# A new written order, engine choice and buffer layout for a four-layer attention kernel

## The chip, the core and the metric

The kernel runs on one core of a Trainium2 chip. The core has five engines that run side by side, each with its own in-order list of instructions: PE (matrix products; its weight loads are listed as PEld), ACT (ScalarE, the only one here that computes exponentials), DVE (VectorE), POOL (GpSimd) and SP (SyncE, which here only issues transfers). An engine waits for another through semaphores. [...] The metric is the device time of one execution in microseconds (us). The kernel before has a median of 419.46 us in three runs (419.31 to 419.74).

## What is computed

Four residual layers on an input of 2048 rows and 512 columns, two kinds of attention in turn, 32 heads of width 16:

```python
x = A_x
x = x + _A_ref(_layernorm(x), A_wqkv, A_wo)
x = x + _B_ref(_layernorm(x), B_wqkv, B_wo)
x = x + _A_ref(_layernorm(x), A_wqkv, A_wo)
x = x + _B_ref(_layernorm(x), B_wqkv, B_wo)

# _A_ref: linear attention
phi = lambda t: jnp.where(t > 0, t + 1, jnp.exp(t)) + 1e-6
kv = einsum("bhsd,bhse->bhde", phi(k), v); z = phi(k).sum(s)
o = einsum(phi(q), kv) / (einsum(phi(q), z) + 1e-6)

# _B_ref: softmax attention over the last 256 positions
scores = q @ k.T * Dh**-0.5, masked to 0 <= i - j < 256
o = softmax(scores) @ v
```

Each kind ends in a product with its `wo`.

## The kernel before

The rows are cut into 16 tiles of 128. A step for one tile is an operation: `s.op(name, {engine: cost}, function, ...)`, which records what it reads and writes. There are 2762 of them on the fast path, and each becomes one instruction or a short run of instructions on one engine. Their names begin with the stage and end with the step.

- `1.` is the key and value half of layer 1: layer norm (`ln.st`, `ln.ag`, `ln.ae` and `ln.xn` on DVE, `ln.rs` on POOL), a transposition `ln.xT`, projections of k and v on PE (`k0`, `k1`, `v0`, `v1`: two halves each), the feature map (`k.e` and `k.r` on ACT, `k.m` and `k.a` on DVE), a copy `vc` of v out of PSUM, and `kv`, the sum over tiles. The transpositions of tiles 0 to 3 run on PE (L834), the others as transfers that SP issues (L827), of 128 KB each.
- `2.` and `3.` are the query halves of layers 1 and 3: `q0`, `q1`, the feature map, the products `n0`, `n1`, the division (`da`, `dr`, `dm` on DVE, L950 to L953), a transposition `o.oT`, the output projection `o.w0`, `o.w1` and the addition `o.x`.
- `2.b.` and `3.b.` prepare layers 2 and 4: layer norm, projections of k, q and v, and copies out of PSUM. A key tile goes out twice, masked for two halves (`kb0`, `kb1`, into kbd, L970), a query tile once (`qc`, into qT, L844), a value tile once (`vc`, into vt, L844); POOL then moves vt into vbd by transfers (`vd0`, `vd1`, L980).
- `2.a.` and `3.a.` are the attention of a tile: products of scores at the border of the window (`sH`, L1006) and inside it (`s0` to `s3`, L1055), their exponentials on ACT (`eH`, L1034; `e00` to `e31`, L1076), masks on DVE (`mH`, L1042; `m0` to `m3`, L1094), products with values (`u`, L1112 and L1124), the division (`dr0`, `dm0` and so on, L1134 and L1136), and the output projection. The last tile of layer 4 has its own ending (`z...`, in `b_end`). `zb` there writes a scaled identity over a part of the zero tile, from which `warm` and `warm2`, products on zeros at the start, read their operands.
- `2k.` is the key and value half of layer 3, worked on while layer 2 still runs.

Most copies out of PSUM may run on ACT or on DVE; the operation lists both. [...]

The order is written out by hand, as it were, in `ORDER`, one word an operation: its number; an apostrophe if it runs on the second engine of its list; and, after a colon, the slots of the buffers that it opens (for PSUM, the bank). `schedule` walks through the words. An engine's instructions stand in the order in which its operations stand there, so the words also fix the sequence in SP's list of transfers and in POOL's. It also adds up a planner's time from the costs in `s.op`; a buffer without a written slot would be placed by it. `emit` then works out the semaphore waits.

Each engine runs a first block of instructions and then branches to a second (`jump`, L504), at the place that `ORDER` gives it.

The loads are issued in `loads` (L774): x tiles and w_Aq on SP, w_Ak and w_Av on ACT, then w_Ao, w_Bk, w_Bq, w_Bv and w_Bo (512 KB each) on SP, at the place in SP's list that `ORDER` gives them.

Of the kernel before, what the change touches and what calls it, by code (L numbers as in the profile page):

```python
# [8 lines left out]
ACT = mybir.ActivationFunctionType  # L9
# [9 lines left out]
ONE = 2.0 ** -9  # L19
# [299 lines left out]
def _act_cost(n):  # L319
    return 0.055 + 0.000833 * n  # L320
# [29 lines left out]
933 476:3 477:3 939:1 672:5.1 673 962:6.0.2 961 686:4.0 963 964 700 487:2.3 488 701 674' 934 702:3 687 688 689 489 490 491:0 492:0 940:5 941 942 943:0  # L350
1019:0.6.2 1020 1021 501 944 690:3.2 691 987 478:2 954:0.4.0 955 956 692' 953 1022 479 678 1416:3.1 1417 716 993:0.6.4 1418' 911:5 912 965 994 995 480 913
1419 966:0.3.5 703:3 967 711:2.2.0 502:6.1 945:1 660 661 957 503 504 505 493:5 494 495 968 969 712 713 997:0.3.1 998 999 506:2 970:5 975:2 971 1054:0.6.0 717
718 719 734 735 972 976 977 1055 1056 752 753 989:0.3.0 679 990 973:2 974:3 978:3 979 1000 704:5.1 988 705 706' 707' 736 708:2.3 737 996 709 710' 714 991 992
1028:0.6.3 1029 1030 1420 1421 720:1 507:3 508:4 1422 693:5.1.1 694 695' 1001:0.2.2 1002 1003 509 510 946:7 947 948 1032:0.5.5 1033 1005:4 1006 1004 1423:2
980:2 1034 738:0 511:7.12.1 1010:3 1433 1434 1435 1007 721:2 1008:0 1009:0 1089:0.5.1 981:2 982 1090 1091 1058 1436 512 1424:0 696 697 515 513 1437:3 770
1411:4.1.0 1412 983 1447 1448 1449 1450 1024:0.5.0 1025 1026 1011 1012 1013:1 1014 1031 726:7.0 727 728' 1413 1414 1415 1063:0.2.4 722:6.2 723 1451:1 1027
# [3 lines left out]
1465 1062 514 740:5.3 741 1075:4 1076 1077 715 1050:3 1092 742 743 1460' 1101 1102:0.2.1 1430:7.2 1103 1104 1431 733 1456 1457 1070 1074 1080:6 1078:0 1079:2  # L360
1159:4.0.0 1160 1161 1432' 747:7.1.2 748 1466 1467:3 749' 1081 1094:2.4.0 1095 1096 1162 1468:3 1082 1083:1 762:7.2 763 1084 1105 764' 773 774:0 1133:0.2.4
1134 1135 516 1085:1 1051:6 1097 1052 1053 765:7.2.4 1477 1106:0.4.2 1107 1108 766 767' 768 758:6.4 759 760' 761' 1137:0.2.5 1138 1139 775:3 1110:7 1111 1109
517:4.2 518 519 520 1112 1113:3 1114:3 1115:6 521:0 1194:0.2.1 1195 1196 1086:7 1087 541:5.13.2 542 545 543 1116 1129:0.2.0 1130 1127 1131 1163 1088 750 751
1136 1491 776:7.5 777 1128 778' 526:5.14.3 527 530 1117 779' 1168:0.2.3 522:2 780:7.3 1118:0 1119 1120:0 528 1132 529 531 781 782' 1478 1479 1480 523:6 524
525 788 1492 789 790 1140 1169 1170 1141:0.4.1 1145:7 1142 1146 1143 1144 1147 1148:1 791 792:1 1149:1 1493 1172:0.2.2 1474:6.7 1469:5.7.0 1475 1173 1476'
793:1 1174 1175 1470 1471 1472 1150:4 769 1229:0.2.2 1230 1231 1121:7 1122 1473 1151 1494 1495:2 1496:4 1481:3 1482:7 1164:0.5.0 1123 1152 1505 1153:3 1154
1171 1165 1166 1167 783:3.0.5 784 532:0.2 794:2.0 1155:3 533 534 535 536:2 1198 1506 1507 1203:4.6.4 785 801:3.1.1 802 803' 1204 1205 1206 795 796 797' 1180:5
1176:0.6.5 1508 1181 1177 556:4.15.1 557 1178 558 1233 1179 1197 560 798:3.0 799 800' 1207:0.6.1 1208 1209 1182 1183:0 1184:0 1185:4 1186 1264:0.2.0 1265 1266
1187 544 546 1188:1 1189 537:1 538:7 539 540 806 1199:0.5.0 1200 1201 807 808 1156:4 1157 1497:7.3.3 1158 1498 1499 1238:0.2.3 1239 1240 1690:6.16.0 1691
1502:5.3 1694 1692 809 810:0 1503 1500 1501 1504' 1202 1190:2 1191:7 1192 1193 1211:0.2.2 1212 1213 1483:5.4.2 1484 1215:4 1521 1242:0.6.5 1243 1244 1216 1217  # L370
811:2 819:3.2.0 1210 1535 1214 1218:3 547:0.2 1219:3 548 559 1536 549 1537 550 551:1 552:0 1485 812:2.1 813 814 815 561 820 821 816:4.1 817 1486 1232 1487
1509:1 1510:9 818' 1234:0.6.0 1235 1538 1539:2 1220:2 1705:3.17.3 1241 1236 1237 1706 1221 1222 1223:0 1224 1709 786 1540:8 2716 1273:0.4.4 1274 1461:7.6 1462
# [995 lines left out]
```

## Time and profile before

| | us |
|---|---|
| median of three runs | 419.46 |
| span of the profiled execution, first to last instruction | 417.1 |
| PE busy | 401.3 |
| ACT busy | 383.3 |
| DVE busy | 379.2 |
| POOL busy | 106.7 |

The profile holds one execution. It gives the span, from the first instruction to the last; the time of a run has some 2.4 us more than that. A group line reads: line of the kernel, engine, operation, what is written and read, shapes, count; then busy time and mean ns of one; then the engine's idle time just before them and what ended it. A line of the view by stage reads: the stretch, its length, then the busy time of PE, PEld, DVE, ACT and POOL with the number of instructions, the clock that PE was granted (1.00 is full), the share of the transfer engines and GB/s. A line of waits reads: who waited, for whom, us in total, times, longest. A line of the chain reads: start, us, what. A line of the timeline reads: start, us, engine and line, what, and in brackets the idle time before it with what ended it. The line of an issue of transfers reads: what, where issued, count, KB each, median us from issue to landing. [...]

### The profile page before, as it was taken

What the parts mean: (1) busy time and instruction counts of PE and PEld (TensorE: products, weight loads), DVE (VectorE), ACT (ScalarE), POOL (GpSimd) and SP (SyncE); (2) the same over time, 40 slices, a digit from 0 to 9 for tenths busy, and PEclk for the clock granted to TensorE, in tenths of its full rate; (3) what the DMA queues carried; (4) which work ended last, traced back from release to release, by engine and by line L of the source; (5) the groups of instructions that cost most, each with busy time, mean ns of one, the idle gap of its engine ahead of it and who ended that gap; (6) DMA issues with size and microseconds to landing.
All of it is one profiled execution on the core that took longest, in us unless ns stands there. A gap on an engine that the chain in (4) does not pass through costs nothing.

```text
span 417.1 us, 18964 instructions
## 1 busy us (share of the span) xinstructions
PE 401.3 (96%) x8402; PEld 283.5 (68%) x8402; DVE 379.2 (91%) x998; ACT 383.3 (92%) x499; POOL 106.7 (26%) x202
## 2 busy tenths in 40 slices
PE   8999999999999999999999999889999999999997
PEld 3654776765767686776686677567676676677775
DVE  6999899999999999999898899999999998979784
ACT  4977979999999999999999677899999999999996
POOL 2331024521343022124150101161333113404100
DMA  8436435343243222324112201331445253243142
GB/s 273 135 63 166 113 53 123 75 55 61 54 77 51 40 48 48 41 53 85 35 40 57 43 2 39 65 81 32 81 66 82 50 72 63 55 85 54 38 93 79
DMA packets 76808, 29.48 MB, mean 71 GB/s; under 512 B 66352, under 2 KB 74672, under 8 KB 76720
## 3 DMA queue, kind: packets, MB, share of 16 engines
q1 hardware_dynamic: 71424, 22.63, 27.0%
q0 software_dynamic: 4096, 4.46, 5.8%
q8 instruction: 68, 1.11, 1.2%
q10 hardware_dynamic: 1200, 1.11, 0.8%
q14 instruction: 20, 0.16, 0.1%
HBM read 6.29 MB, written 2.10 MB: 20 GB/s over the span
## 4 chain that ended last, share of the span: by engine, by line
ACT 47%; PE 41%; DVE 10%; issue 1%; DVEq 0%
ACT pF L1076 33%; PE ps L857 17%; ACT pH L1034 9%; PE ps L869 8%; PE ps L1055 4%; PE ps L1124 4%; PE ps L1112 2%; PE ps L915 2%; ACT kbd L970 2%; DVE o L953 1%; DVE xres L892 1%; DVE stats L813 1%; ACT E L878 1%; PE ps L1253 1%; ACT vt L844 1%
## 5 line engine op out<-in xcount | busy, mean ns | idle before, releaser
L1076 ACT ACTIVATE pF<-ps 128x1024 bf16<-128x1024 f32 x240 | 231.0, 1095 | 2.7 <-PE ps L1055 2.0
L817 POOL TENSOR_TENSOR rstd<-mv,const 128x1 f32<-128x1 f32 x64 | 39.7, 622 | 208.9 <-DVE mv L816 200.1
L980 POOL DMA_DIRECT2D vbd<-vt x128 | 67.0, 532 | 81.1 <-DVE vt L844 61.6
L1034 ACT ACTIVATE pH<-ps 128x1024 bf16<-128x1024 f32 (+1 forms) x64 | 60.5, 1032 | 3.1 <-PE ps L1006 3.0
L1124 PE MATMUL ps<-vbd,pF 128*128 128x34 bf16 x1856 | 59.6, 178 | 0.0
L1124 PEld LDWEIGHTS ps<-vbd,pF 128*128 128x128 bf16 x1856 | 52.9, 96 | 3.3 <-issue 0.2
L1055 PE MATMUL ps<-qT,kbd 32*128 32x128 bf16 x1920 | 49.0, 216 | 4.4 <-ACT pF L1076 1.2
L1094 DVE TENSOR_TENSOR pF<-pF,const 128x512 bf16<-128x512 bf16 (+2 forms) x116 | 46.7, 414 | 4.8 <-ACT pF L1076 4.6
L878 ACT ACTIVATE E<-ps 128x512 bf16<-128x512 f32 x64 | 39.5, 635 | 8.4 <-PE ps L857 4.3
L813 DVE BATCH_NORM_STATS2 stats<-xres 128x6 f32<-128x512 bf16 x64 | 43.8, 687 | 1.9 <-DMA xres<-in_A_x_dram 1.1
L1055 PEld LDWEIGHTS ps<-qT,kbd 32*128 32x128 bf16 x1920 | 28.7, 92 | 22.8 <-ACT pF L1076 9.4
L1042 DVE TENSOR_TENSOR pH<-pH,const 128x1024 bf16<-128x1024 bf16 (+1 forms) x64 | 40.8, 650 | 0.0
L857 PE MATMUL ps<-w_Bv,xT 128*128 128x512 bf16 (+2 forms) x152 | 35.7, 346 | 0.3 <-ACT vt L844 0.2
L869 PE MATMUL ps<-xT,w_Bk 128*128 128x128 bf16 x512 | 35.3, 219 | 0.3
L869 PE MATMUL ps<-xT,w_Bq 128*128 128x128 bf16 x512 | 35.2, 219 | 0.1
L857 PE MATMUL ps<-w_Ao,oT 128*128 128x512 bf16 (+2 forms) x144 | 34.5, 356 | 0.7 <-ACT pF L1076 0.6
L1112 PEld LDWEIGHTS ps<-vbd,pH 128*128 128x128 bf16 x928 | 28.6, 96 | 8.8 <-issue 1.8
L857 PE MATMUL ps<-w_Ak,xTa 128*128 128x512 bf16 (+1 forms) x134 | 33.6, 369 | 0.6 <-ACT xTa L844 0.5
L869 PE MATMUL ps<-xTa,w_Aq 128*128 128x128 bf16 x512 | 33.9, 219 | 0.2
L1112 PE MATMUL ps<-vbd,pH 128*128 128x34 bf16 x928 | 32.9, 178 | 1.1 <-ACT pF L1076 0.3
L857 PE MATMUL ps<-w_Bo,oT 128*128 128x512 bf16 (+2 forms) x140 | 33.0, 355 | 0.7 <-ACT pF L1076 0.6
L857 PE MATMUL ps<-w_Av,xTa 128*128 128x512 bf16 (+2 forms) x133 | 33.6, 371 | 0.0
(95 smaller groups left out, 622.4 us busy)
## 6 DMA issues: line engine op xcount, KB each, us to landing
vbd<-vt POOLq DMA_DIRECT2D x128, 34.0 KB, 2.1
xres<-in_A_x_dram SPq DMA_DIRECT2D x16, 128.0 KB, 4.9
out_dram<-xres SPq DMA_DIRECT2D x15, 128.0 KB, 1.9
oT<-o SPq DMA_TRANSPOSE x60, 2.6
w_Ak<-in_A_wqkv_dram ACTq DMA_DIRECT2D x1, 512.0 KB, 4.8
w_Av<-in_A_wqkv_dram ACTq DMA_DIRECT2D x1, 512.0 KB, 5.8
w_Aq<-in_A_wqkv_dram SPq DMA_DIRECT2D x1, 512.0 KB, 6.2
w_Ao<-in_A_wo_dram SPq DMA_DIRECT2D x1, 512.0 KB, 4.0
```

Of the source, the lines that this page charges most:

```text
L813: s.op(n + ".st", {"DVE": 0.595}, lambda e, en: e.bn_stats(a_st, x.h[:]), reads=[x], writes=[st])
L857: i = e.matmul(g.h[:, a:b], xT.h[:, kt, :], w.h[:, kt, a:b], start=(kt == 0), stop=(kt == 3), skip_group_check=True)
L869: i = e.matmul(g.h[:, f * P:(f + 1) * P], w.h[:, kt, f * P:(f + 1) * P], xT.h[:, kt, :], start=(f == 0 and kt == 0), stop=(kt == 3), skip_ ...
L878: s.op(n + ".e", {"ACT": _act_cost(512)}, lambda e, en: e.activation(E.h[:], g.h, ACT.Exp, bias=0.0), reads=[g], writes=[E])
L980: return [e.dma_start(vbd.h[64 * a:64 * a + 64, j, a], vt.h[64 * j:64 * j + 64, a]) for j in range(2)]
L1034: return e.activation(d, c, ACT.Exp, bias=0.0, scale=DH ** -0.5)
L1042: return e.tensor_tensor(v, v, tr, ALU.mult)
L1055: i = e.matmul(ss[r // 2].h[:, r % 2, k * P:k * P + P], kbds[fj[m] // 2].h[32 * r:32 * r + 32, f, fj[m] % 2, :], qT.h[32 * r:32 * r + 32, ...
L1076: s.op("e%d%d" % (u, g), {"ACT": _act_cost(1024)}, lambda e, en, S=ss[g], pb=pb, g=g: e.activation(pb.h[:, 2 * g:2 * g + 2, :], S.h, ACT.E ...
L1094: return e.tensor_tensor(v, v, tr, ALU.mult)
L1112: i = e.matmul(U.h[:, c:c + 34], pH.h[:, 4 * r + f, 64 * a:64 * a + P], vbds[j // 2].h[:, j % 2, :, 4 * f + r, :], start=first[0], stop=Tr ...
L1124: i = e.matmul(U.h[:, c:c + 34], pFs[at[f, m][0]].h[:, r, at[f, m][1] * P:at[f, m][1] * P + P], vbds[fj[m] // 2].h[:, fj[m] % 2, :, 4 * f ...
```

## The change

The operations and what they compute stay. `ORDER` is written anew, all 2762 words, after a local search on a replay of the schedule:

```diff
 ORDER = """
-4 2 37 38 66 6 0 61:7 1 7 8 9 41 68 42 43 44 45 69 70 46 5 3 71 72:0 73:6.0 47 62 67 39 40 74 85 86 87 88 10 75:7.0.0 76 11 12 89:1 33 25 90:6.1 91 13 102
...
-2717:3 2726 2660 2661 2695 2696 2751:7.3 2697 2734 2735 2736 2743 2745 2744 2589 2752 2753 2755 2756 2754 2758 2759 2757 2760 2761
+0 6 7 1 5 3 67 4 2 39 37 8 9 38 66 41 42 43 44 61:7 45 46 47 48 49 68 69 70 40 71 72:0 85 35 73:6.0 62 33 50 51 52 53 54 55 56 57 58 59 74 75:7.0.0 86 87 88
...
+2755 2754 2758 2759 2756 2757 2760 2761
 """
```

Three costs and one dependency change beside it:

```diff
-        s.op("dr", {"DVE": 0.17}, lambda e, en: e.reciprocal(dn.h[:], dn.h[:]), writes=[dn], tail=0.11)
+        s.op("dr", {"DVE": 0.275}, lambda e, en: e.reciprocal(dn.h[:], dn.h[:]), writes=[dn])
...
-            s.op("kb%d" % a, {"ACT": _act_cost(512), "DVE": _dve_cost(512)}, kb, reads=[gk, self.mab], part=[kbd])
+            s.op("kb%d" % a, {"ACT": 0.57, "DVE": 0.659}, kb, reads=[gk, self.mab], part=[kbd])
...
-        s.op("zb", {"DVE": 0.2}, lambda e, en: e.tensor_scalar(big.h, self.ident.h[:], LIFT / ONE, None, op0=ALU.mult), reads=[self.ident, self.zero], writes=[big])
+        zb = s.op("zb", {"DVE": 0.2}, lambda e, en: e.tensor_scalar(big.h, self.ident.h[:], LIFT / ONE, None, op0=ALU.mult), reads=[self.ident, self.zero], writes=[big])
+        for d in s.ops:
+            if d.name in ("warm", "warm2"):
+                zb.deps[d] = False
```

(`_act_cost(512)` is 0.48 and `_dve_cost(512)` 0.598.)

What the new list does, read from the two lists engine by engine:

- Of PE's 975 operations 804 stand at another place, most by a few places (median 2, farthest 28); of DVE's about 990, 898 (median 6, farthest 378: `zb`, from the middle of the kernel to its first stage).
- 27 copies go from ACT to DVE and 21 from DVE to ACT; ACT has 497 operations instead of 503, DVE 999 instead of 993.
- 487 of 687 placements in PSUM banks differ, and 443 others.
- SP's list: before, the four loads of w_Ao, w_Bk, w_Bq and w_Bv stand behind the twelve transpositions of stage `1.` that SP issues; after, they stand ahead of them, right behind the last load of an x tile. w_Bo stands behind the first five of these transpositions instead of behind the first transpositions of `2.`.
- The branch of DVE stands 42 operations before its end instead of 12; POOL's is its 29th operation instead of its 110th; ACT's stays near its 295th.
- PE changes between row groups and square products 304 times instead of 302.

More of the change, by code (lines that the diff above doesn't have):

```diff
@@ L352 @@
[L352 to L355, printed above, removed]
@@ L363 @@
[L363 to L366, printed above, removed]
@@ new lines @@
+886 605' 403:7 404 418:6 915 65 865:0.2.0 426 405 864 419 644 631:3 632:7.3 633 916 420 634' 866 867 892:0.4.1 639:6.2.5 427:2.3 428 640 893 894 635' 442:0.1
[4 rows of a table added]
+919:0.5.0 926 882 1405 986 930 448:4 449 920 958:2.0.3 921 1406 675:7.2.2 676 672:6.1 959 960 450 931:2.4.1 932 677' 673 472:0.2 473 922 698 474 933 935:7 475
[3 rows of a table added]
+753 713' 1054:0.6.0 754 1055 502:2.0 503 976 1421 734 704:5.1 705 1056 977 504 505 506:2 735 989:0.2.0 990 991 706' 693:7.1.4 694 978:3 707' 946:6 979
+1028:0.4.3 1422 679 947 695' 1423:1 1029 736 708:7.3 709 992 1001:0.2.2 507:2 948 996 1030 1002 1003 508:6 509 710' 1005:7 1032:0.4.5 1000 1433 510 1004 1006
@@ new lines @@
+1007 720:0 1010:6 1033 1034 1008:1 1009:1 1434 1435 1022 770 771 1424:1 1057 980:1 1089:0.2.1 714 981:7 982 1090 1091 1011 1024:0.4.0 1012 755 737 772 1031
+1023 1013:2 511:3.12.2 512 983 1014 721:2 1436 1437:3 1447 1025 1026 729:2.2.0 730 731' 1063:0.4.4 722:7.2 723 1411:6.6.3 515 513 1027 1064 1065 1015:3 1438:2
+1036:0.2.1 1037 1412 756:2 1448 1449 726:5.0 727 1425:4.5.0 1426 1413 1038 1427 738:1 724' 725' 1414 1415 1039 1040:7 1067:0.2.2 773 1439:6.4.1 1450 732 1440
+1041 1068 728' 1035 1428 1069 696 733 1045:5 1451:0 1441 1042 1429 1043:0 1124:0.2.2 715 697 757:4 1046 1125 1126 1442 514 1443 739:0 1444:4.7 1445 1044:0
@@ new lines @@
+1070 1047 1452:5 1066 1059:0.6.0 1060 1061 1446' 744:3.1 1016:2 1017 1048:3 1049 1058 1098:0.4.3 1093 1099 1100 745 1018 746' 1128 1463 1464 1050:0 740:7.3
+741 1062 1453:6.2.3 742 743' 1071:0.2.5 1072 1073 1458:5.3 1459 1465 1454 1460' 1075:4 1455 1076 1102:0.2.1 1466 1103 1074 1456 1457 1077 1078:1 1079:2 516
+1104 1080:7 1081 1159:0.5.0 1160 1082 765:4.2.5 766 1083:2 1105 1084 1467:3 1161 1094:0.2.0 767' 1095 1096 1163 1430:7.2 1085:2 762:6.2 1101 1092 1431
+1133:0.4.4 1134 763 747:3.0.1 748 1135 1051:2 749 750 751 1052 1106:0.4.2 1097 1432' 764' 774:2 1468:4 775:1 517:6.0 1053 518 1107 1108 758:3.4 759 1110:2
@@ new lines @@
+1111 760 519 520 521:3 1137:0.6.5 1138 1139 1112 1477 1109 1115:5 1116 1478 761' 1194:0.3.1 1113:3 1479 1114:1 1136 522:1 1195 1117 1162 1118:1 1119 780:2.3
+781 1196 523:7 1129:0.5.0 524 782 1120:3 1130 1140 1086:4 1087 1168:0.2.3 1131 1480 525 788 1088 1169 1170 776:7.5 1481:1 777 1482:3 1469:6.1.0 1141:0.4.1
+1470 541:3.13.1 789 1132 778' 779' 1127 542 783:2.1.2 784 1142 1471 1143 1491 1472 790 785' 1492 791 1145:7 1144 792:0 1473 1172:0.4.2 1146 1147 1148:2 543
+545 1197 1149:0 786 1198 1173 1174 526:3.14.3 527 1150:2 1493 1494 787 1151 1229:0.4.2 530 528 1152 1121:3 1122 1230 1231 1175 1164:0.6.0 1165 544 768 1153:0
@@ new lines @@
+1154 529 1171 1495:3 1123 556:2.15.2 1474:5.1 1475 531 1203:0.3.4 557 1166 1476' 1204 558 1205 1505 532:6.3 533 793:3 1496:8 534 535 798:5.0 799 794:1.0 795
+1155:0 1506 536:2 1176:6.3.5 801:0.0.4 537:1 802 1177 1178 1507 800' 1167 560 1180:5 1181 1182 1508 796' 797' 1179 1207:6.3.1 803' 1183:1 1184:3 1208 1232
+1185:2 1186 1187 1188:2 1264:0.6.0 1189 1509:2 1190:2 538:5 539 1206 1209 1265 1502:4.5 1199:0.2.0 540 806 807 1503 1266 1156:5 1157 1200 1201 1238:0.6.3
+1504' 804 546 769 805 1191:4 1192 1158 1239 1240 1497:5.7.0 1498 1210 1202 1215:3 1211:0.6.2 1499 1521 808 1193 1483:2.3.3 1212 1213 1705:4.16.1 1706 1216
@@ new lines @@
+1217 1707 1709 1242:0.6.5 1484 1522 1243 1510:6 1244 1500 809 1535 810:1 1523 1536 811:2 1501 1537 547:4.0 548 559 1218:3 1219:1 1524 1538 561 1690:3.17.0
+1214 549 1691 1692 1694 1485 819:1.1.3 820 1220:0 550 551:0 552:3 1234:4.6.0 812:3.1 1221 813 1222 1233 821' 1539:0 1235 1236 1486 1487 1273:4.1.4 1540:7 1274
+1223:1 1241 1275 1461:7.6 1224 814' 816:0.1 562:4.2 563 1245 817 1225:1 1462 815 564 565 553:1 1246:2.6.1 554 818 1226:0 1227 1237 1247 1248 1525:3 566:2
+1299:2.4.1 555 824 1511:1.0.2 1512 1780:7.0.3 1781 1228 825 826 1526:13 567:0 1250:6 1251 822 823 827 1549 1300 1301 1513 1550 1693 1514 1515 1551 1277:2.4.2
@@ new lines @@
+1933 2199 1959 1742 2200 1901' 2203:0.2.0 1960 2182 1945:0 1743 1744 1745:2 1934 2204 2205 1961 1962:2 1928:7.0 1929 1930' 1732:6 2207:0.4.1 2208 2209 1963:4
+1733 1931' 1734 2214 1935:3.0.4 1936 1756:0.0 1757 1758 2206 1759 1950:2.3 1746:0 1976 1937 1760:3 2243:4.6.4 1964:3.1 1902 2244 2245 1965 2230:4.0.0 2231
+2232 1951 1952 1921 1903 2183:7 1747:6 1748 2184 2185 2188:5 2189 2190 1761:2 1966' 2202 1977 1967' 1978 2210 2233 2235:0.3.2 2236 2186:2 2201 2191:1 1979
+1938 1749 1939 2187:0 2192 1946:2.2 1947 2239:0.6.5 2237 1948' 1949' 2240 2241 1968:5.0 2215:4 1969 2234 2266:2.0.1 2216 2217 1762:7 1763 2238 1970' 2242
@@ new lines @@
+2218:3 2219:1 2267 1980:1 1873 1764 2279:2.5.0 1981:3 2268 2280 2281 2251:4 1845 2252 2253 2254:0 2255:2 2247:0.2.2 2012 2248 2249 1994 1953:7.1.0 1771:5.2
+1772 1773 2246 1971:4.2.1 2193:3 1995 1954 1955 1956 2013 1972 2271:0.2.5 2250 1774 2256:7 2257 2272 2273 2258 1775:3 1973' 1858 2259:1 2275:0.5.4 1982:4.3
+1983 1996 2260 2270 2276 2277 2220:7 2302:0.2.0 2303 1984' 1985' 2304 1997 2221 2222 2223:3 2224 1776:1 1777:6 1778 2315:0.4.2 2316 2317 2014 1957 2015 2274
+1779 1986:7.1 1987 2283:2.0.1 2269 2284 2285 1988' 1860 2318 1786:6.0 1787 1788 1789 2225:0 1790:0 1989:5.0.3 2226:4 1990 1791:2 1801:2.2 1802 1991 2278
[4 rows of a table added]
@@ new lines @@
+2387:0.2.5 2388 2389 2068 2027' 2328:4 2300 2049 2354 2050 2010 2033 2069 1831:6.1 1832 2028 1833 1834 1835:3 2018:5.5 2019 2020 2377 2021 2329 2330 2331:3
+1836:0 2379:0.2.2 2380 2342 1822:7 1823 2332 2029 2011 2381 2022:6.3 2355:0.4.0 2346 2034:2 1824 2350 2023 1837:3 1838 2024' 2382 2356 2357 2410:0.6.0 2051
[4 rows of a table added]
+1869 2400:4 2401 2427:0.2.5 2414 2402 2403:1 2428 2426 2462 2404 2058:7.1 2059 2451:0.5.4 2369:1 1881:2 2060' 2429 2449 2450 2087 2431:4 2432 2433 2434:3 2452
+2105 2106:3 2107:2 2453 2405:0 2455:0.2.0 2456 2457 2076:7.2 2077 1882:6 2435:3 2430 2078' 2482:0.4.1 1883 2138 2088:2 1884 2061:7.2.0 2062 2483 2484
[4 rows of a table added]
@@ new lines @@
+2507:0 2502 2526 2112:3.0 2529 2408 2113 2114' 2535:0.4.0 2536 2537 2508:2 2509 2510 2567:0.6.2 2557 2521 2568 2569 2373 2441:2 2161:0 2108:3.4 2109 2511:0
+2512 2538 2100 2082 2083 2110' 2544:2 2559:0.4.3 2125:4 2409 2545 2560 2570 2561 2133:7.2.2 2130:6.1 2131 2132' 2111 2101 2477:1 2134 2563:0.4.4 2564 2546
+2565 2135' 2530 2334:3 2335 2558 2336 2143:3 2513:0 2566 2603:0.6.0 2604 2539:5 2540 2590:0.3.1 2541 2605 2151:7.0.5 2562 2547:2 2542:1 2543:2 2548 2591 2592
+2152 2153' 2154 2136 2571:0.5.1 2115:2.1.4 2116 2572 2117' 2594 2126:7.5 2595:0.3.5 2127 2575:2 2573 2576 2596 2597 2599:0.5.3 2577 2128' 2129' 2144:7.0 2145
@@ new lines @@
+2578:3 2606 2579:3 2574 2600 2626:0.3.0 2601 2146' 2147' 2148:2.2 2149 2580:5 2627 2639:0.6.4 2581 2593 2150' 2598 2602 2137 2628 2442:4 2640 2582 2583:0 2641
+2607:0.2.2 2549:3 2608 2443 2609 2630 2584 2444 2118 2478:7 2479 2642 2631:0.5.1 2632 2119 2611:4 2612 2613 2337 2635:0.2.5 2633 2610 2480 2636 2514:7
+2169:6.2.0 2170 2637 2614:1 2615:1 2585:2 2515 2662:0.4.2 2155 2171 2663 2664 64 2162:3.2 2163 2516 2164' 2616:2 2675:0.6.3 2617 2618 2676 2634 2677 2165'
+2619:2 2629 2620 2643:4.0.0 2166:3.3 2167 2644 2645 2550:2 2638 2168' 2667:4.6.2 2551 2647:3 2665 2666 2668 2669 2648 2445 2621:1 2671:0.4.1 2552 2672 2673
[3 rows of a table added]
```

53 lines of the change are left out of this document (8 added, 45 removed), and 94 rows, old and new, of the table ORDER.

## The prediction

> **What bounds the kernel now.** I read the page's busy times first, then busy times by stage, then the waits and the chain.
>
> ```profile
> PE 401.3 (96%) x8402; PEld 283.5 (68%) x8402; DVE 379.2 (91%) x998; ACT 383.3 (92%) x499; POOL 106.7 (26%) x202
> 0.00:58.50 58.50, 56.14 (x466) 33.26 (x467) 52.47 (x175) 44.24 (x77) 12.68 (x29) 1.00 0.50 136
> 58.50:222.30 163.80, 159.73 (x3593) 114.81 (x3594) 154.51 (x394) 160.26 (x201) 48.06 (x89) 1.00 0.32 59
> 222.30:263.60 41.30, 40.49 (x650) 29.15 (x649) 37.93 (x107) 31.80 (x52) 3.99 (x6) 1.00 0.21 40
> 263.60:417.08 153.48, 144.97 (x3698) 106.27 (x3698) 134.24 (x325) 147.04 (x170) 42.00 (x78) 1.00 0.36 66
> ```
>
> Columns two to six of a stage are its length and the busy times of PE, PEld, DVE, ACT and POOL. I cut at the first border product (L1006) of layer 2, at that of its last tile, and at the first of layer 4. In stage one PE sets the pace, in stage two ACT (160.3 of 163.8 us) with PE at its heels, in the handover PE with DVE, in the last stage ACT again. No engine has an eighth of the span to give away on average, but each stage has a different tightest one, so each shift of work is priced in its stage.
>
> ```profile
> PEld ps L1055 <- ACT pF L1076: 9.4, 34, 0.5
> PEld ps L1006 <- ACT pF L1076: 3.9, 12, 0.8
> PEld ps L1055 <- ACT pH L1034: 2.9, 11, 0.6
> PEld ps L941 <- ACT pF L1076: 2.7, 7, 0.5
> ```
>
> These are PE's weight loads waiting for exponentials: 64 waits of 0.3 us, 18.9 us in all. The order can win only what lies in such short waits.
>
> ```profile
> 7.03 1.02 PE ps L857 x4
> ...
> 12.98 0.22 PE ps L834 x4
> 13.20 0.86 PE ps L857 x4
> 14.06 0.89 PE ps L869 x16
> 14.96 2.69 PE ps L857 x12
> 17.65 0.47 PE ps L915 x8
> ```
>
> From 12.98 to 18.12 the chain is PE piece after piece without a gap: any hole made in PE in stage one is paid in full.
>
> **The change, part by part.** *Copies.* 27 copies go from ACT to DVE and 21 back. Counted between the same cuts in the two orders, stage two loses 5 kbd copies and 3 plain ones (qT, vt, vA together) on ACT.
>
> ```profile
> 197.07 0.98 ACT vA L844 x2
> 201.72 1.14 ACT kbd L970 x2
> L970 DVE TENSOR_SCALAR kbd<-ps,const 128x512 bf16<-128x512 f32 x40 | 28.2, 742 | 0.5 <-PE ps L869 0.4
> L844 DVE CAST qT<-ps 128x512 bf16<-128x512 f32 x22 | 15.0, 682 | 0.9 <-PE ps L869 0.8
> ```
>
> Back to back on ACT a kbd copy takes 0.57 us and a plain one 0.49: 5 x 0.57 + 3 x 0.49 = 4.3 us less. On DVE each costs at most its mean of one, 0.74 and 0.68. DVE's net gain there is only about 1.5 us, because other DVE work leaves the stage; 154.5 + 1.5 still fits under 160.
>
> *PE pieces.* Stage two also loses two half projections (L857, 0.86 for four matmuls, so 0.43 a half) and three value products of 16 matmuls; the handover gets those five and gives half a query projection (L869, 0.89 for 16, so 0.45) to the last stage.
>
> ```profile
> 216.23 0.81 PE ps L1124 x32
> ```
>
> A value product is 0.40, so stage two loses 2 x 0.43 + 3 x 0.40 = 2.1 us of PE work and the handover gains 2.1 - 0.45 = 1.6. ACT could shorten stage two by 4.3, PE by 2.1; I take the middle, -3.2. The handover is PE's: +1.6. The last stage gets one exp and one relu of a query and one copy more on ACT, less a small one, about +1.1 by 0.49 each, and 0.45 on PE; ACT is idle 6.4 us there, so +0.9.
>
> *Weight loads.* This decides. Before, SP issued twelve transposes, then the loads of w_Ao, w_Bk, w_Bq and w_Bv. After, those four stand right behind the last load of xres and ahead of every transpose (w_Bo follows five transposes).
>
> ```profile
> 9.92 0.43 SPq L774 DMA_DIRECT2D xres<-in_A_x_dram  x1
> xres<-in_A_x_dram SPq DMA_DIRECT2D x2, 128.0 KB, 4.3
> 12.29 1.30 SPq L827 DMA_TRANSPOSE xTa<-xn  x1
> xTa<-xn SPq DMA_TRANSPOSE x1, 4.1
> 36.14 0.58 SPq L774 DMA_DIRECT2D w_Ao<-in_A_wo_dram  x1
> 37.87 0.51 SPq L774 DMA_DIRECT2D w_Bv<-in_B_wqkv_dram  x1
> w_Ao<-in_A_wo_dram SPq DMA_DIRECT2D x1, 512.0 KB, 4.0
> w_Bv<-in_B_wqkv_dram SPq DMA_DIRECT2D x1, 512.0 KB, 6.3
> q1 hardware_dynamic: 71424, 22.63, 27.0%
> ```
>
> The issue costs little: four loads take 36.14 to 38.38 = 2.2 us of SP, and between 10.35 and 12.29 SP is empty. The transfer is another matter. The last xres lands at 9.92 + 4.3 = 14.2. The four weights land at 40.1 to 44.2, three steps in 4.1 us, 1.36 us each, so behind xres they end at 14.2 + 4 x 1.36 = 19.6. All of SP's transfers share one queue: 22.6 MB in q1 only fits if the transposes are in it with loads and stores. Does a transpose wait behind a bulk load there? The nearest case is w_Bo:
>
> ```profile
> 65.50 0.57 SPq L774 DMA_DIRECT2D w_Bo<-in_B_wo_dram  x1
> w_Bo<-in_B_wo_dram SPq DMA_DIRECT2D x1, 512.0 KB, 4.8
> 66.13 2.31 SPq L827 DMA_TRANSPOSE oT<-o  x1
> oT<-o SPq DMA_TRANSPOSE x1, 4.6
> xTa<-xn SPq DMA_TRANSPOSE x27, 2.6
> ```
>
> w_Bo lands at 70.3. The transpose issued right behind it, at 66.1, took 4.6 us instead of the usual 2.6 and landed at 70.7, 0.4 later; the first of all, behind xres, took 4.1 and landed at 16.4, 2.2 after xres. So I take the queue to be in order. [...] Behind four loads the first transpose lands at 19.6 + 0.4 to 19.6 + 2.2, so 20.0 to 21.8. It carries tile 4, whose first projection stands in the new order behind 15 half projections of k or v, 6 of q, three L834 groups and one L915 group: 15 x 0.43 + 6 x 0.45 + 3 x 0.22 + 0.24 = 10.05 us after the first k projection, which starts at 7.03, so due at 17.1. PE is empty for 2.9 to 4.7 us. Some comes back: PE sits without work for 2.4 of stage one's 58.5 us now, and DVE, which it waits for there, runs ahead meanwhile. I take +3.3, inside the lower half for that; bounds 0 (transposes pass the loads) and +4.7.
>
> *At nothing.* The new durations of dr, kb0 and kb1 only feed the planner, whose order, engines and banks are written out: no instruction. zb (0.19 us) moves into stage one, where DVE has 6 us idle; with that cover gone, 0.2. The new waits for warm and warm2 hold nothing: both stand ahead of PE's first projection at 7.03. Two more changes between square and row-tiled matmuls:
>
> ```profile
> L1055 PEld LDWEIGHTS ps<-qT,kbd 32*128 32x128 bf16 x1920 | 28.7, 92 | 22.8 <-ACT pF L1076 9.4 <-issue 4.7 <-ACT pH L1034 2.9
> ```
>
> 22.8 us over 120 groups is 0.19 each, hidden or not: 0.2 at most.
>
> *DVE's branch* moves from 12 to 42 DVE instructions before the end, with o.x and the last kbd copies queued behind it and PE's scores waiting for those.
>
> ```profile
> L504 DVEq COMPARE_BRANCH  x1: 53/53/53, 407.2 to 407.2; - x1
> 407.14 0.42 DVE L1136 SCALAR_TENSOR_TENSOR o<-dn,ps 128x256 bf16<-128x256 f32 x1
> 410.12 0.21 DVE L1175 RECIPROCAL dn<-ps 128x8 f32<-128x8 f32 x1 [2.56 <-PE ps L1166]
> 388.00:394.00 6.00, 5.90 (x142) 3.84 (x140) 4.27 (x9) 6.00 (x8) 0.00 (x0) 1.00 0.18 46
> ```
>
> The branch takes 0.05 us, the hole after it is 2.56 and is put down to PE, so its price lies between 0.05 and 2.6. DVE is idle 1.7 of 6 us at the new place; 0.9 could stick out. I take 0, since the hole has another releaser. [...]
>
> *Order as such.* 804 of PE's 975 steps and 487 of 687 bank placements differ. No row prices this. The 18.9 us of short waits bound it: a fifth won is -3.8, a sixth lost +3.2. I take -1.5, nearer the middle than either, on the gain side because the kbd copy that the old plan held for 0.48 us reads 0.57, and work planned behind it had to come late.
>
> Sum: +3.3 - 3.2 + 1.6 + 0.9 - 1.5 = +1.1 on a span of 417.1. The median 419.46 is 2.4 above that span, and I leave this part as it is: 419.46 + 1.1 = **420.6 us**.
>
> **Rivals.** *The transposes pass the weight loads.* Then the 3.3 falls out: 417.3. For it: one late transpose near w_Bo coincides with POOL's transfers too. Against: 22.6 MB in one queue.
> *PE takes the loss back.* PE's order has enough tile-0-to-3 work, stage two falls by the full 4.3 and the waits by 3: 3.3 - 4.3 + 1.6 + 0.9 - 3.0 = -1.5, 418.0. For it: ACT's 160.3 of 163.8.
> *It evens out.* Hole 2.8 instead of 3.3, waits -2.2: -0.1, 419.4.
> *DVE becomes the bound in the handover.* Already it is busy 37.9 of 41.3 there, and 3.3 us of DVE work (layer norm steps, two kbd copies, adds) come in. If DVE sets that stage, +3.3 stands for +1.6 and stage two gains only PE's 2.1: 3.3 - 2.1 + 3.3 + 0.9 - 1.5 = +3.9, 423.4. It decides once DVE's idle time there, 3.4, is used up. [...]
>
> **Chances.** Forecast 0.40, DVE bound 0.10, evens out 0.16, PE takes it back 0.16, transposes pass 0.18. Within 0.2% (0.84 us, about what can be told apart here) is 418.6 to 420.3. So slower 0.50, same 0.16, faster 0.34. Range 416.2 to 423.4; the forecast's own, by the hole's 2.9 to 4.7 and 1 us of order to either side, 419.2 to 423.0.
>
> **What would show it.** Right: after some 17 us PE idles about 3 us, put down to the transpose's DMA or to DVE; w_Ao is issued at 10.4; the first transpose lands past 20; stage two is 2 to 4 us shorter, the handover longer. Wrong: PE stays full from 10 to 46 us (then 417.3), or the hole after DVE's branch holds up scores near 390, or DVE reads 99% in the handover.

## The result and the profile after

The changed kernel takes 433.27 us (median of four runs, 432.76 to 434.14) against 419.6 for the kernel before on the same chip: a ratio of 1.0327, 95% interval 1.0309 to 1.0345. The forecast was 420.6, range 416.2 to 423.4. Slower was right; the size was not nearly. The profiled execution's span grows from 417.1 to 431.2, by 14.1 us. (The later runs of the kernel before list spans of 417.0 to 419.5 us, 1.3 below their times, so a stage's change of less than about 1 us can lie between executions.)

The page of the changed kernel, its busy times, its granted clock by slices and its chain by engine:

```profile
PE 395.5 (92%) x8325; PEld 285.9 (66%) x8395; DVE 376.4 (87%) x1004; ACT 381.5 (88%) x493; POOL 108.2 (25%) x202
...
PEclk9979999999999999999999999999999999999998
...
PE 38%; ACT 29%; DVE 19%; DMA 11%; issue 2%; SPq 1%; DVEq 0%
```

PE, ACT and DVE are busy a little less than before and each has a smaller share. (PE's record lacks 77 matmuls, 8325 of 8402, so its busy time is understated.) A new owner stands in the chain: transfers, with 11%. The same kernel by stage, cut at the same four PE products as in the prediction (columns as there):

```profile
0.00:64.20 64.20, 57.71 (x464) 34.55 (x472) 49.56 (x173) 45.58 (x79) 13.11 (x29) 0.95 0.53 132
64.20:227.90 163.70, 153.51 (x3513) 113.86 (x3541) 153.52 (x394) 156.84 (x194) 47.58 (x85) 1.00 0.32 56
227.90:270.80 42.90, 41.45 (x689) 30.50 (x698) 39.93 (x113) 30.11 (x49) 5.58 (x10) 1.00 0.21 37
270.80:431.20 160.40, 142.88 (x3673) 106.99 (x3698) 133.38 (x327) 149.00 (x172) 41.97 (x78) 0.99 0.33 64
```

| stage | before | after | change | forecast |
|---|---|---|---|---|
| one | 58.5 | 64.2 | +5.7 | +3.3 |
| two | 163.8 | 163.7 | -0.1 | -3.2 |
| handover | 41.3 | 42.9 | +1.6 | +1.6 |
| last | 153.5 | 160.4 | +6.9 | +0.9 |
| order as such, all stages | | | in the above | -1.5 |

Where PE waits points to why. The view of waits of the changed kernel (who waited, for whom: us in total, times, longest); the line numbers are one higher than before:

```profile
PEld ps L858 <- DMA oT<-o: 10.3, 13, 1.6
PE ps L858 <- DMA oT<-o: 5.9, 8, 1.6
PEld ps L858 <- DMA xTa<-xn: 4.6, 2, 4.3
PE ps L858 <- DMA xTa<-xn: 3.8, 1, 3.8
PEld ps L870 <- DMA xT<-xn: 3.4, 3, 1.6
PE ps L870 <- DMA xT<-xn: 3.0, 3, 1.4
```

PE's matmuls wait 5.9 + 3.8 + 3.0 = 12.7 us for SP's transposes (PEld's lines are mostly the same waits, seen by the weight loads). In the kernel before there is not one such line. All lines of PE in this view add up to 28.5 us, against 10.1 before, 18.4 more; its waits for ACT shrink from 5.3 to 2.8 meanwhile. Another 5.9 of the 28.5 read "issue", against 0.2 before. Those look like gaps in the record rather than waits: the traces of this case that hold 8312 to 8326 of PE's matmuls all have 4.3 to 6.1 us of them, those that hold 8394 to 8402 at most 1.6. So the changed order won some of what the forecast had looked at, and lost more elsewhere.

The transposes themselves hardly changed. The view of tile oT, on the kernel before and then on the changed one (duration of the issue in ns, smallest, median, largest; then who waited; then issue to landing):

```profile
L827 SPq DMA_TRANSPOSE oT<-o x60: 1188/1192/2665, 46.1 to 407.6; - x60
...
who waited for it (us, times):
...
DMA to landing us min/median/max: 2.4/2.6/5.2
```

```profile
L828 SPq DMA_TRANSPOSE oT<-o x60: 1188/1264/2636, 54.1 to 419.9; - x60
...
who waited for it (us, times):
  PEld ps L858: 10.3, 13
  PE ps L858: 5.9, 8
...
DMA to landing us min/median/max: 2.4/3.0/5.1
```

In both kernels the fastest of oT lands after 2.4 us and the slowest after 5.1 or 5.2. Of all 117 transposes 37 took over 3.3 us before and 44 after: about a third, whichever order. What differs is how closely PE follows. Matched one by one in the trace, from the landing to PE's first weight load that reads it, one transpose in 117 was used within 0.35 us before, 24 after; the median margin fell from 3.2 to 2.4 us. The planner's time (`LAT["SP"]`) makes a transpose readable 1.45 us after its issue of about 1.25 has ended, 2.7 in all. A search on that time may place PE's step at exactly 2.7. Of the 117, 72 before and 64 after land within 1.45 us of the end of their issue; for the others the margin must pay. The planner's own time shows the packing. Added up by `schedule` from each kernel's words and costs, it is 412.9 us for the kernel before, where no transpose is planned to be read within 0.35 us of becoming readable, and 408.7 for the changed kernel, where 19 are. It is 408.7 with the loads at either place, so it knew nothing of the queue either.

What goes with a late landing can be read from the packets in the trace. Beside SP's queue the page lists one of instruction transfers, packets of 16 KB (queue, packets, MB, share):

```profile
q8 instruction: 68, 1.11, 1.1%
```

In the kernel before, one of these was under way between 1.0 and 2.4 us after the issue of 44 transposes; 32 of these 44 took over 3.3 us, of the other 73 only 5. In the changed kernel it is 36 of 52 with one and 8 of 65 without. Over all fifteen traces of this case it is 494 of 691 with, and 80 of 1039 without. This is a coincidence in time: no run changed the instruction transfers.

In stage one the forecast hole is there. SP's timeline of the changed kernel, and PE's:

```profile
10.90 0.43 SPq L775 DMA_DIRECT2D w_Ao<-in_A_wo_dram  x1
...
12.48 0.92 SPq L775 DMA_DIRECT2D w_Bv<-in_B_wqkv_dram  x1
14.08 9.55 SPq L828 DMA_TRANSPOSE xTa<-xn  x5
```

```profile
7.78 1.04 PE L858 MATMUL ps<-w_Ak,xTa 128*128 128x512 bf16 x4 [0.66 <-DMA w_Ak<-in_A_wqkv_dram]
...
17.64 0.59 PE L858 MATMUL ps<-w_Ak,xTa 128*128 128x512 bf16 x2
22.02 1.89 PE L858 MATMUL ps<-w_Av,xTa 128*128 128x512 bf16 x4 [3.79 <-DMA xTa<-xn]
```

The first transpose, issued at 14.08, lands 7.9 us later (the chain has `14.08 7.90 DMA xTa<-xn`), and PE stands empty from 18.23 to 22.02. (Some 0.75 us of stage one's loss stand ahead of all this: the first k projection starts at 7.78 instead of 7.03, behind a wait for w_Ak, which is issued ahead of the moved loads.) What came behind the hole was not forecast. The windows 20 to 24, 24 to 30 and, within these, 20.7 to 27.4 us of the changed kernel:

```profile
20.00:24.00 4.00, 1.89 (x4) 0.73 (x6) 1.96 (x6) 0.00 (x0) 0.79 (x1) 0.58 1.32 102
24.00:30.00 6.00, 5.87 (x35) 3.16 (x35) 2.29 (x11) 3.15 (x7) 1.06 (x2) 0.71 0.36 99
...
20.70:27.40 6.70, 5.16 (x15) 2.24 (x17) 2.32 (x7) 1.04 (x2) 0.79 (x1) 0.50 0.82 147
```

From 24 to 30 PE is busy 5.87 of 6 us at a granted clock of 0.71 on average; before, it was 1.00 there. In the trace the clock is at half from 20.64 to 27.46 and full on both sides. From 22 to 32 us a v projection's matmul takes 507 ns on average, 379 before, and a k projection's 454, 378 before. The hole costs its own length and then some 2.7 us of slow matmuls, an estimate from these 11 and 17 matmuls.

### The profile page after: what moved, and what is told of

The parts are those of the page before. It is cut to its first block, busy times and chain, and to the rows that moved or that the text cites. A ratio compares the mean times of both kernels' runs of the same rounds, so it can differ in the third digit from the quotient of the medians.

```text
span 431.2 us, 18871 instructions
## 1 busy us (share of the span) xinstructions
PE 395.5 (92%) x8325; PEld 285.9 (66%) x8395; DVE 376.4 (87%) x1004; ACT 381.5 (88%) x493; POOL 108.2 (25%) x202
## 3 DMA queue, kind: packets, MB, share of 16 engines
q0 software_dynamic: 4096, 4.46, 5.6%
## 4 chain that ended last, share of the span: by engine, by line
PE 38%; ACT 29%; DVE 19%; DMA 11%; issue 2%; SPq 1%; DVEq 0%
ACT pF L1077 21%; PE ps L858 16%; PE ps L870 7%; DMA oT<-o 6%; ACT pH L1035 5%; PE ps L1125 5%; PE ps L1056 4%; DVE stats L814 2%; PE ps L1113 2%; DVE o L954 2%; DMA xT<-xn 2%; DMA xTa<-xn 2%; DVE xres L893 2%; PE ps L916 2%; DMA w_Ak<-in_A_wqkv_dram 1%
## 5 line engine op out<-in xcount | busy, mean ns | idle before, releaser
L818 POOL TENSOR_TENSOR rstd<-mv,const 128x1 f32<-128x1 f32 x64 | 41.3, 647 | 202.6 <-DVE mv L817 196.6
L1125 PE MATMUL ps<-vbd,pF 128*128 128x34 bf16 x1856 | 61.0, 178 | 0.9 <-issue 0.9
L1125 PEld LDWEIGHTS ps<-vbd,pF 128*128 128x128 bf16 x1856 | 53.9, 96 | 5.3 <-issue 1.2
L858 PE MATMUL ps<-w_Av,xTa 128*128 128x512 bf16 (+1 forms) x129 | 34.0, 380 | 4.5 <-DMA xTa<-xn 3.8
L858 PE MATMUL ps<-w_Ao,oT 128*128 128x512 bf16 (+2 forms) x124 | 29.6, 350 | 7.7 <-DMA oT<-o 4.9
L858 PE MATMUL ps<-w_Bo,oT 128*128 128x512 bf16 (+2 forms) x126 | 30.7, 352 | 5.0 <-DVE pF L1095 1.4
L870 PE MATMUL ps<-xTa,w_Aq 128*128 128x128 bf16 x512 | 35.1, 219 | 0.0
L971 DVE TENSOR_SCALAR kbd<-ps,const 128x512 bf16<-128x512 f32 x45 | 32.2, 740 | 2.5 <-PE ps L870 2.3
L858 PE MATMUL ps<-w_Ak,xTa 128*128 128x512 bf16 (+1 forms) x118 | 32.2, 385 | 2.1 <-issue 0.8
```

Source lines behind the costliest of these rows:

```text
L818: s.op(n + ".rs", {"POOL": 0.53}, lambda e, en: e.tensor_tensor(a_rs, v, self.half.h[:], ALU.pow), reads=[mv, self.half], writes=[rs])
L858: i = e.matmul(g.h[:, a:b], xT.h[:, kt, :], w.h[:, kt, a:b], start=(kt == 0), stop=(kt == 3), skip_group_check=True)
L870: i = e.matmul(g.h[:, f * P:(f + 1) * P], w.h[:, kt, f * P:(f + 1) * P], xT.h[:, kt, :], start=(f == 0 and kt == 0), stop=(kt == 3), skip_ ...
L1125: i = e.matmul(U.h[:, c:c + 34], pFs[at[f, m][0]].h[:, r, at[f, m][1] * P:at[f, m][1] * P + P], vbds[fj[m] // 2].h[:, fj[m] % 2, :, 4 * f ...
```

## The experiments

Two theories stood against each other for what the loads don't explain. *Late transposes*: PE was packed at the planner's 2.7 us behind them, so each late one stops it. The rivals: the new choice of engines, POOL's transfers in the same memory, DVE's branch, or durations that the planner had wrong.

**The loads.** In the changed order they go back; in the old order they go forward.

```diff
 ORDER (loads_back, from the changed kernel; w_Bo, 60, moves back too)
-54 55 56 57 58 59 74 75:7.0.0 ... 317:15 310' ... 631:3 632:7.3
+54 55 74 75:7.0.0 ... 317:15 56 57 58 59 310' ... 631:3 60 632:7.3
 ORDER (loads_early, from the kernel before; w_Bo, 60, moves forward too)
-95 55 334 18 97 ... 370 56 57 58 59 357:0
+95 55 56 57 58 59 334 18 97 ... 370 357:0
```

> The changed kernel with the five wo/wqkv loads back at their old places in SP's list (four behind the twelve transposes of stage 1., w_Bo later), all else as changed. If the loads made the hole in stage one (4.17 us at 22.0) and the half-clock matmuls behind it (2.2 us), stage one falls from 64.2 to about 58.5 with PE's clock at 1.00, and the time from 433.3 to 426.5 to 428. By the prediction's own price of the hole alone (3.3) it is 430. If the new order would have made PE wait there anyhow, it stays above 431.5. In each case the loss of the last stage (6.9) stays, since it hangs on no load.

> The kernel before with the loads at the places that the change gives them (four behind the last x tile, w_Bo behind five transposes), all else as before. If the queue is in order, the first transpose lands at 21 to 22 instead of 16.4 and the time is 423 to 425.5 (hole of 3 to 4 us, clock dip 0 to 2). If the transposes pass the loads, 419 to 420.5.

With the loads back: 426.45 us (425.42 to 427.5), ratio to the kernel before 1.0156 (1.0122 to 1.0191). That is 6.8 less than the changed kernel, stage one is down from 64.2 to 57.1, and the last stage stays at 161.9. With the loads forward in the old order: 424.05 (420.77 to 425.07), ratio 1.0114 (1.0085 to 1.0143), so 4.7 more than the 419.34 of its comparison. Transposes waited behind the loads in both orders: the first one landed 7.9 us after its issue in the changed order and 7.4 in the old one (`13.58 7.41 DMA xTa<-xn` in its chain), against 4.1 in the kernel before. The early loads cost 6.8 us in the changed order and 4.7 in the old one; why they differ was not tested.

The four runs with the loads forward also show the clock. PE's timeline of its profiled execution:

```profile
21.03 0.60 PE L863 MATMUL ps<-w_Ak,xTa 128*128 128x512 bf16 x2 [2.21 <-DMA xTa<-xn]
```

Here the hole is 2.21 us and the clock stayed at 1.00: 420.8 us. The other three runs had a mean clock of 0.996 and took 423.5 to 425.1; the holes in these are not on record.

The length of one hole does not decide it. In the traces half clock comes for 3.41 us or twice that. In the run with the loads back such a stretch (301.84 to 305.25) follows a hole of 1.49 us, while in `before_engines_of_after` (below) a hole of 2.85 us at 178.28 is followed by none. PE's busy share in the 3.41 us ahead fits better. Each trace is cut into steps of 3.41 us, counted from its changes of clock; the shares are those of the matmuls on record. From 10 us on, each of the ten steps in which PE was busy 47.3% or less is followed by half clock (in the changed kernel 17.23 to 20.64, 30%), and none of the six with 47.5 to 52% is; the run with the loads forward has 47.5% around its hole. Five more half-clock stretches in the last 13 us of a run follow shares of 59 to 70%, so this is not the whole rule.

**POOL's transfers**, in the changed kernel:

```diff
-return [e.dma_start(vbd.h[64 * a:64 * a + 64, j, a], vt.h[64 * j:64 * j + 64, a]) for j in range(2)]
+return [e.dma_start(vbd.h[64 * a:64 * a + 4, j, a], vt.h[64 * j:64 * j + 4, a]) for j in range(2)]
```

> The changed kernel with POOL's transfers of vt into vbd cut from 64 rows to 4 (most of vbd keeps its preset values, so the result isn't the reference's). If these transfers are what makes SP's transposes land at 3.5 to 4.3 us instead of 2.5, PE's waits for transposes outside stage one (about 19 us) fall by half or more: 421 to 427. If the transposes are late by themselves, or by each other, 431 to 434.5.

430.94 (429.04 to 434.04), ratio 1.0255 (1.0215 to 1.0295). The page gives the queue of these transfers 0.29 MB instead of 4.46, in the same 4096 packets; the waits stay:

```profile
PE ps L863 <- DMA oT<-o: 7.0, 8, 1.4
PE ps L863 <- DMA xTa<-xn: 4.8, 1, 4.8
PE ps L875 <- DMA xT<-xn: 2.4, 3, 1.3
```

The time is just under the 431 that was said for transposes late by themselves, and the run leaves most of vbd at its preset values. 40 of 117 transposes still took over 3.3 us, 36 of them among the 49 with an instruction transfer under way. The bytes of POOL's transfers are not what makes a third of them late. Their number of packets was not changed, so that stays open; the instruction transfers are the nearest candidate, and not tested.

**The choice of engines**, in the kernel before: 48 words gain or lose their apostrophe, for instance `214` for `214'`; nothing is moved. (In the traces of both kernels 882 instructions read PE's products out of PSUM: 493 on ACT and 389 on DVE before, 487 and 395 after, none on another engine.)

> The kernel before with the changed kernel's choice of engine for the 48 copies (27 from ACT to DVE, 21 from DVE to ACT), order, slots and loads as before. If the choice is what the changed kernel loses by (DVE too full in the handover and the last stage), the time is 424 or more. If it is worth the 1 to 3 us that stage two was to gain by it, 416.5 to 418.5. If the loss is in the order of PE and the transposes alone, within 2 us of 419.5.

450.3 (448.59 to 452.25), ratio 1.0747 (1.0712 to 1.0782). By its letter this is the first outcome, 424 or more. But 31 us is over twice what the changed kernel lost, so it says little of the change. The planner's own time rises here from 412.9 to 440.0, too: a copy that goes to another engine's list at the old place stands in front of work that an order written for the old choice wants first. Only a choice together with its order can be priced.

**The margin itself.** I searched the order anew by local moves on a replay of the same schedule, four times: from the changed order with its loads back, and from the old order, each with a transpose readable 1.45 us after its issue has ended, and with 2.0 to 3.0. Copies had their durations from the trace. In the searches with 2.0 to 3.0, POOL's moves of vt into vbd were also told as 0.8 us later in the late case. Slots stay, steps move within their engine, some 30 copies change engine; 354 to 493 of PE's 975 steps move, by one or two places mostly.

```diff
 ORDER (all words, searched with a transpose readable ... us after its issue)
-1.45            (tight_from_after, tight_from_before)
+2.0 to 3.0      (slack_from_after, slack_from_before)
```

> ORDER searched anew from the changed order with its loads back, slots kept, copies at their measured durations, and a transpose planned to be readable 1.45 us after its issue ends, as the planner of both kernels has it (in the traces it is 1.2 us for most and 2 to 4 for a third). Theory 'late transposes': PE is packed as closely behind them as in the changed order, a fifth of them is used within 0.35 us of landing, PE waits 15 us or more for them, 422 to 430. Rival 'the durations were wrong' (a search with measured durations repairs the order by itself): 414 to 419.

> The same start and the same search, but a transpose planned to be readable 2.0 to 3.0 us after its issue ends (vd moves 0.8 us later in the late case). 'Late transposes': under a tenth is used within 0.35 us of landing, PE's waits for them fall under 8 us, 413 to 420, and 5 us or more below the search with 1.45. Rival 'durations': within 2 us of the search with 1.45. Rival 'the changed banks and slots hold PE, whatever the order': 423 or more.

> The same search with 1.45 us from the order before, its loads and slots kept. 'Late transposes': the margin of the old order is spent, slower than the kernel before, 421 to 428. 'Durations': 413 to 418.

> The same search with 2.0 to 3.0 us from the order before, its loads and slots kept. 'Late transposes': the margin stays (at most 5 transposes used within 0.35 us of landing) and what the search wins elsewhere is kept: 415 to 419, faster than before. If a search on these costs wins nothing on the chip at all, 419 to 422.

| | us (lowest to highest) | ratio to before (95%) | PE waits for transposes | used within 0.35 us |
|---|---|---|---|---|
| before | 419.1 | 1 | 0 | 1 |
| loads_back | 426.45 (425.42 to 427.5) | 1.0156 (1.0122 to 1.0191) | 11.6 | 22 |
| tight_from_after | 431.17 (429.43 to 433.82) | 1.0273 (1.0241 to 1.0305) | 10.3 | 24 |
| slack_from_after | 421.14 (419.96 to 423.75) | 1.0046 (1.0027 to 1.0066) | 2.3 | 8 |
| tight_from_before | 422.65 (421.96 to 423.77) | 1.0078 (1.0058 to 1.0099) | 4.0 | 18 |
| slack_from_before | 421.83 (420.51 to 424.56) | 1.0066 (1.0039 to 1.0093) | 1.6 | 6 |

(The fourth column adds the waits of PE's matmuls for oT, xT and xTa.) From the changed order the latencies that were told differently make 10 us, 8.0 of them in PE's waits for transposes; each search was made once. PE's waits in the tight search and then in the one with slack:

```profile
PE ps L863 <- DMA oT<-o: 4.4, 5, 1.6
...
PE ps L875 <- DMA xT<-xn: 3.3, 4, 1.7
...
PE ps L863 <- DMA xTa<-xn: 2.6, 3, 1.5
```

```profile
PE ps L875 <- DMA xT<-xn: 1.3, 2, 0.9
...
PE ps L863 <- DMA oT<-o: 1.0, 2, 0.8
```

This is the 'late transposes' outcome, with three bounds missed (slack took 421.1 where at most 420 was expected; tight took 431.2 where at most 430 was, and waited 10.3 where 15 was). "The durations were wrong" falls: the tight search had durations from the trace and came out slower than what it started from. From the old order the difference is only 0.8, and the intervals overlap: there the margin matters less. The one with slack was to be faster than the kernel before (415 to 419) and was not, so both searches lost some 3 us by something else. They had been told trace durations, which may hold time that the written costs count elsewhere; this was not tested by itself, but the next runs went back to the written ones.

**PE's list alone**, from the changed order with its loads back: 269 steps move, median one place, the other four lists untouched.

> The changed order with its loads back, and only PE's list searched again with transposes readable 2.0 to 3.0 us after their issue: 269 of 975 steps move, most by one place, SP, ACT, DVE, POOL and all slots untouched. 'Late transposes, and PE stands too close behind them': PE's waits for transposes fall by a third or more and the time by 2 to 5 us, from 426.5 to 421.5 to 424.5. If the transposes' sources or the work of ACT and DVE are what is late, so that PE's list can't help: 425.5 to 428.

425.12 (423.72 to 426.9), ratio 1.0153 (1.0127 to 1.018). PE's waits for transposes fell from 11.6 to 4.4 us, but the time by 1.3, and the intervals overlap. Its waits for ACT rose from 2.7 to 5.2. So a wait for a transpose that is taken away does not come back as time one for one, and the packing was not undone in PE's list alone; perhaps what produces the transposes, and what ACT and DVE do meanwhile, was laid out for it too. The theory in its narrow form missed.

**DVE's branch**, in the kernel before and then in the changed order with its loads back:

```diff
 ORDER (branch_early, from the kernel before: word 64 goes 30 places up in DVE's list)
-2443 2444 2445 ... 2714 2409 64 2625
+2443 64 2444 2445 ... 2714 2409 2625
 ORDER (loads_branch_back, from loads_back: word 64 goes down to 12 before the end)
-2663 2664 64 2162:3.2 ... 2708 2723:3
+2663 2664 2162:3.2 ... 2708 64 2723:3
```

> The kernel before with DVE's branch 42 instead of 12 places before its end, as in the changed kernel, and nothing else. If the hole behind the branch (2.56 us before, 2.40 after) belongs to what DVE waits for, no change: 418.5 to 420.2. If it is the branch's own, up to 0.9 is added: 420 to 421. If it also keeps o.x and the last kbd copies from PE in a stretch where PE has nothing else, 421 to 422.5.

421.15 (420.73 to 423.43), ratio 1.0063 (1.0039 to 1.0086): 2.0 us slower, and 2.1 of them in the last stage (153.5 to 155.6). DVE's timeline there, and PE's:

```profile
393.05 1.29 DVE L899 SCALAR_TENSOR_TENSOR xres<-ps,xres 128x512 bf16<-128x512 f32 x2 [2.32 <-issue]
```

```profile
393.88 1.05 PE L875 MATMUL ps<-xT,w_Bq 128*128 128x128 bf16 x16 [2.16 <-DVE xres L899]
```

The hole follows the branch, and now its releaser reads "issue": nothing that the profile shows. It is the branch's own. The kernel's planner charges for it, in both kernels: `s.op("jump", {e: 2.9}, ...)`. PE, which needs the bank that `o.x` frees, waits 2.16 of DVE's 2.32 us. Then in the changed order:

> The changed order with its loads back and DVE's branch back at 12 places before its end, all else as changed. If the branch costs here what it cost in the order before (2.0), 424 to 425. If in the changed order PE waits for transposes in that stretch anyway and the branch hides behind that: 426 to 427.5. What then remains above the kernel before is the order's own.

427.06 (425.33 to 429.58), ratio 1.0204 (1.0174 to 1.0233), against 426.45 with the branch where the change put it. No gain. At the place where the change put it, DVE's hole is there (2.39 us in the run with the loads back), but PE has other work behind it: between 394 and 399 us it waits 0.2 us in all. At the old place DVE's hole is 2.68 us in this order, and PE waits 2.1 of it. So this run took no cost away, and it is the trace of the run with the loads back that shows the branch to be no part of the loss.

**A search with the third that is late.** Written costs (kb0, kb1 and dr as changed), and the mean over six draws in which two of three transposes are readable 1.25 to 1.35 us after their issue has ended and the third 1.9 to 3.2:

> The same search from the order before with loads and slots kept, but on the written costs (kb0, kb1 and dr as changed) instead of durations read from the trace, and on the mean over six draws in which two of three transposes are readable 1.25 to 1.35 us after their issue and the third 1.9 to 3.2, as the traces have them. 'Late transposes, and nothing else is wrong with such a search': at most 5 used within 0.35 us of landing, faster than before, 416 to 418.5. If what a search wins is lost to other things as well (as in the run with 2.0 to 3.0 from before, 421.8): 419 to 422.

> The same with the changed order, its loads back and its slots as the start. 'Late transposes': near the search with 2.0 to 3.0 from there, 417 to 421.5. If only the wide margin of that search helped, 423 or more.

From the order before: 417.7 us (415.43 to 419.16), ratio 0.9961 (0.9943 to 0.9978): faster than both kernels, though by 1.4 us only. Its waits for transposes:

```profile
PE ps L875 <- DMA xT<-xn: 0.7, 1, 0.7
PE ps L863 <- DMA xTa<-xn: 0.3, 1, 0.3
```

Seven transposes were used within 0.35 us (at most five were expected), and PE's own waits are 9.6 us in all, against 10.1 before. From the changed order with its loads back: 418.94 (417.85 to 422.15), ratio 1.001 (0.9988 to 1.0031), no different from the kernel before and 7.5 below its own start. This order keeps all banks and slots of the changed kernel and 38 of its 48 changed copies, so these don't stand in the way. Between these two searches and those with 2.0 to 3.0 both the costs and the latencies changed, so which of the two helped is open.

## Why the prediction was wrong

- *Loads, +3.3.* The mechanism was right in each step: in-order queue, first transpose past 20 us (21.98, where 20.0 to 21.8 was said), PE empty for 2.9 to 4.7 (3.79 as the timeline puts it). The size was off. I took back some of the hole for slack in stage one and priced nothing behind it; the hole came to 3.79 in full, and the clock fell. Stage one lost 5.7; taking the loads back won 7.1 there (64.2 to 57.1, which is 1.4 below the old stage) and 6.8 in all. Half clock came with this hole of 3.79 us and not with the one of 2.21. But it set in at 20.64, 2.41 us into the hole, and in the run with the loads back behind a hole of 1.49, so the length of the hole alone does not explain it. A price for slow matmuls belonged into the sum beside the hole; the old trace, at 1.00 throughout, has no row of it.
- *Stage two, -3.2.* The work did leave: ACT is busy 156.84 there instead of 160.26. The stage stayed at 163.7. The freed time became waits of PE: 2.9 us for transposes, against none, and 2.1 for DVE, against 0.4. (The durations of DVE's copies that I took were upper bounds: in the old trace 706 of 998 records of DVE begin before the one ahead has ended, by 0.08 us in the median.)
- *Handover, +1.6.* Measured +1.6, in part by luck: 0.8 of it are waits for transposes, and PE is busy only 0.96 longer.
- *Last stage, +0.9.* Measured +6.9. With the loads back it is still 8.4 longer than before (161.9), with the slack search 2.6 (156.1). The largest part is PE's wait for transposes, 5.1 us there; a second half-clock stretch (423.41 to 426.82) is in it as well.
- *Order as such, -1.5, bounds -3.8 and +3.2.* This is the step that failed. All terms without the loads were forecast at -2.2, and the changed order with its loads back is 7.1 above the kernel before. I bounded the term by the waits that the old profile shows, PE's short ones for exponentials (and took the 18.9 us of its weight loads, which overlap its matmuls, 283.5 us of loads and 401.3 of matmuls in a span of 417.1; PE's matmuls waited 5.3 for ACT). Waits that the old order had no line of can't be seen in that list. What the profile did show was the spread of the transposes: "xTa 2.6" as a median, with single ones at 4.1 and 4.6 quoted beside it. I read these as signs of the bulk loads, not as the tail of every transpose, and never asked how far PE stood behind them.
- *The branch at nothing.* Right in the sum, by cover; wrong in the reason. The 2.56 us were put down to PE by the profile and I believed it, though the kernel's text charges 2.9 for a branch. Moved in the old order, the hole came along and cost 2.0. The record of the branch is one of 53 ns, which tells nothing of the hole behind it.
- *The rivals.* DVE as the bound of the handover didn't come: it is busy 39.93 of 42.9 there. Transposes that pass the loads are refuted by both runs on the loads. The other two counted on gains that did not come.

The sum as measured: 6.8 for the loads and the clock behind them (433.27 to 426.45), and 7.5 that a search with the late third gave back (426.45 to 418.94), which leaves nothing between that kernel and the one before. The second term is the order's as a whole. Of its parts it is shown that the latency told to the search matters (10 us between the searches with 1.45 and with 2.0 to 3.0 from the changed order, 0.8 from the old one) and that POOL's bytes and DVE's branch don't. That the waits for transposes make up all of the 7.5 is not shown: taking 7.2 us of them away in PE's list alone won 1.3. Why a third of the transposes lands late stays open, but for its coincidence with the instruction transfers.

## What to carry to other kernels

Ask of each wait that the profile does not show how many us it has in hand: for a transfer, from landing to first use, against the spread of its landings and not their median. An order searched on one fixed latency may spend all margin beyond it, so give the search the spread. A bulk load put ahead of small transfers in one queue is late work for whoever reads these (here the first transpose landed 7.9 us after its issue behind four loads, instead of 4.1), and a hole in PE can be paid for again in clock: here behind steps of 3.41 us in which PE was busy 47.3% or less, 30% in the changed kernel.

## What the runs showed that I had not expected

- A branch of DVE leaves a hole behind itself: 2.56, 2.40, 2.39 and 2.32 us where I looked for it near the end, and between 1.6 and 3.0 in all fifteen traces. In most of them the profile names for it whatever DVE would have waited for next.
- A third of SP's transposes takes over 3.3 us from issue to landing instead of some 2.5 (the median of the others is 2.48 in the traces of both kernels), in each order (35 to 44 of 117 wherever all landings are known), with POOL's transfers at a sixteenth of their bytes too; most of these had an instruction transfer under way.
